# A second level inside product 5 of the last unit of a seven-product matmul kernel

## The chip, the cores and the metric

One core of one Trainium2 chip. The time is device microseconds of that core, the median of several executions.

Times **counted from the first matmul of the last unit** are called "of the unit" below.

## The reference

```python
# x0: [16384, 1024] bf16, ws: [6, 1024, 1024] bf16, bs: [6, 1024] bf16
x = x0
for l in range(6):
    proj = jnp.einsum('bd,de->be', x, ws[l]) + bs[l]
    x = x0 * proj + x
return x
```

## The kernel before

The batch is cut into 16 pairs of blocks of 512 rows. With six layers that makes 96 units (pair, layer). Each unit is one product of 1024 x 1024 by 1024 x 1024, done as a two by two block product with seven half-size products instead of eight (Winograd's form). In 89 units products 5 and 2 are again done by that form (the "second level", seven inner products of a quarter size each). The first pair and the last unit have one level only.

An entry of a rank table, such as `P5.0@6.9`, gives an operation a wished time; a list scheduler orders the instructions of each engine by it. `P` is a group of four matmuls that sum into one bank of PSUM (the memory that TensorE writes), `E` and `F` are ScalarE evacuations of such banks (`F` into another bank), `Q, U, V, W` are the four output quadrants.

```python
def group(name, w, bank, bname, rhs, rname, m, start, u=u):
    def fn():
        for k in range(KH):                                    # KH = 4
            nc.tensor.matmul(bank[:], lhsT=wt[(u, w)][:, k, m * P:(m + 1) * P], rhs=rhs[:, k, :],
                             start=(start and k == 0), stop=(k == KH - 1), skip_group_check=True)
# ... (one: a unit with one level; pA, pX: four PSUM banks each)
for m in range(KH):
    group(f"P1.{m}", "1", pA[m], A[m], B11, [XI[0, 0]], m, True)
    if one:
        copy(f"F1.{m}", pX[m][:], pA[m][:], [A[m]], [Xn[m]])           # product 1 into product 2's bank
        group(f"P2.{m}", "2", pX[m], Xn[m], B21, [XI[1, 0], Xn[m]], m, False)
        biased(f"E2.{m}", Q[:, m, :], pX[m][:], 0, m, [Xn[m]], [f"Q.{m}"])
        group(f"P5.{m}", "5", pX[m], Xn[m], T[1], ["T1"], m, True)
        copy(f"E5.{m}", P5s[:, m, :], pX[m][:], [Xn[m]], [f"5c.{m}"])
# ... second level: inner products on 256 columns in two banks a, b, with ScalarE between them
inner(5, b, True)
copy(X + "e_p5", ip5[X][:], v3(b), [Xn[b]], [X + "ps"])
inner(1, a, True)
copy(X + "f1", pX[b][:], pX[a][:], [Xn[a]], [Xn[b]])
inner(2, b, False)
copy(X + "e_c11", c(0, 0), v3(b), [Xn[b]], cn(0, 0))
inner(6, a, False)
copy(X + "f2", pX[b][:], pX[a][:], [Xn[a]], [Xn[b]])                  # must end before inner 7 writes bank a
inner(3, b, False)
copy(X + "e_c12", iu[X][:, 0], v3(b), [Xn[b]], [X + "u0"])
inner(7, a, False)
# ...
```

In the last unit there is an output stage. Q and the two halves of U are transposed by DMA from the SyncE queue and stored by GpSimd. V and W are transposed on TensorE, evacuated, and stored by four DMAs, the last of them (half of W) from ScalarE's queue.

Of the kernel before, what the change touches and what calls it, by code (L numbers as in the profile page):

```python
# [137 lines left out]
Ua0@16.6 Um0@17.2 Ux0@17.8 Ua1@18.4 Um1@19 Ux1@19.6 Va0@20.4 Vm0@21 Vx0@21.3 Va1@21.6 Vm1@22.2 Vx1@22.8  # L138
Wm0@22.9 Wm1@23.7 Wm2@24.6 Wm3@25.4 cW.0@26.3 cW.1@26.5 cW.2@26.7
trQ@19 stQ@20 trU0@20.5 trU1@22.5 stU0@24 stU1@26 stVa@27 stVb@27.5 stWa@28 stWb@29  # L140
""")}
SPAN2, SPAN0 = 23.4, 24.2

# [2 lines left out]
def kernel(  # L146
# [12 lines left out]
    KH = KD // 2  # L159
# [18 lines left out]
    pA = [psum.tile([P, NB], FP32, name=f"pA{i}") for i in range(KH)]  # L178
    pX = [psum.tile([P, NB], FP32, name=f"pX{i}") for i in range(KH)]
    x0Ts = [work.tile([P, 2, KD, NB], BF16, name=f"x0T{i}") for i in range(2)]  # L180
    xsts = [work.tile([P, 2, KD, NB], BF16, name=f"xst{i}") for i in range(2)]
    T = {i: work.tile([P, KH, NB], BF16, name=f"T{i}") for i in (1, 2, 3, 4)}
# [3 lines left out]
    P1s, P5s, Q, U, V, W = (work.tile([P, KH, NB], BF16, name=f"ev{i}") for i in range(6))  # L186
# [7 lines left out]
    def blk(t, dh, n):  # L194
        return t[:, n, dh * KH:(dh + 1) * KH, :]
# [15 lines left out]
    level1 = lambda u: units[u][0] == 0 or u == NU - 1  # L211
# [3 lines left out]
    for u, (pr, l) in enumerate(units):  # L215
        if pr == 0:
            ring_seq += [(u + 1, w, k) for w, k in RAW if l < L - 1] + [(u, w, k) for w, k in MAKE]
        else:
            order = "1 2 5 6 7 3 4" if level1(u) else "1 5 5i 2 2i 6 3 7 4"
            ring_seq += [(u, w, "load") for w in order.split()]  # L220
    wt, uses_left, live = {}, {}, []
    pos = {"next": 0}
# [44 lines left out]
    for u, (pr, l) in enumerate(units):  # L267
        one, first, last = level1(u), u == 0, u == NU - 1
# [5 lines left out]
        XI = X0 if l == 0 else XO  # L274

        def add(name, fn, rd=(), wr=(), weights=(), rk=rk, base=base, u=u):
            op(base + rk[name], fn, rd, wr, [(u, w) for w in weights])
# [4 lines left out]
        def group(name, w, bank, bname, rhs, rname, m, start, u=u):  # L282
            def fn():
                for k in range(KH):
                    nc.tensor.matmul(bank[:], lhsT=wt[(u, w)][:, k, m * P:(m + 1) * P], rhs=rhs[:, k, :],  # L285
                                     start=(start and k == 0), stop=(k == KH - 1), skip_group_check=True)
            add(name, fn, rname + [f"w{u}.{w}" + ("a" if name in ("P5.0", "P5.1") and u == 0 else "")] if pr == 0 else rname, [bname], [w])

        def copy(name, dst, src, rd, wr):
            add(name, lambda: nc.scalar.copy(out=dst, in_=src), rd, wr)  # L290

        def biased(name, dst, src, eh, m, rd, wr, l=l):
            c = l * KD + eh * KH + m
            add(name, lambda: nc.scalar.activation(out=dst, in_=src, func=IDENT, bias=b_all[:, c:c + 1], scale=1.0), rd, wr)  # L294

        late = []
        if pr == 0:
# [32 lines left out]
            for X, s in (("2i", isum[2 * (l % 2)]), ("5i", isum[2 * (l % 2) + 1])):  # L330
                a = lambda r, c, X=X, u=u: wt[(u, X[0])][:, r * KQ:(r + 1) * KQ, c * HQ:(c + 1) * HQ]
                sv = s[:].rearrange("p q (k e) -> p q k e", k=KQ)
                rn = lambda i, X=X, l=l: f"{X}{l % 2}.{i}"
                src = [f"w{u}.5"] if X == "5i" else []
# [9 lines left out]
        B11, B12, B21, B22 = blk(xs, 0, 0), blk(xs, 0, 1), blk(xs, 1, 0), blk(xs, 1, 1)  # L344
# [3 lines left out]
        ttop("T4", T[4][:], B21, T[2][:], SUB, [XI[1, 0], "T2"], ["T4"])  # L348
        A = [f"A{m}" for m in range(KH)]
        Xn = [f"X{m}" for m in range(KH)]  # L350
        if not one:
            for X, Bm, src in (("5", T[1][:], "T1"), ("2", B21, XI[1, 0])):
                q = lambda dh, n, Bm=Bm: Bm[:, dh * KQ:(dh + 1) * KQ, n * NQ:(n + 1) * NQ]
                t_ = tin[X]
                ttop(X + "t13", t_[:, 0:2], Bm[:, :, NQ:NB].rearrange("p (d k) b -> p d k b", d=2),
                     Bm[:, 0:KQ, :].rearrange("p k (n b) -> p n k b", n=2), SUB, [src], [X + "t13"])
                ttop(X + "t2", t_[:, 2], q(1, 1), t_[:, 0], SUB, [src, X + "t13"], [X + "t2"])
                ttop(X + "t4", t_[:, 3], q(1, 0), t_[:, 2], SUB, [src, X + "t2"], [X + "t4"])
        for m in range(KH):
            group(f"P1.{m}", "1", pA[m], A[m], B11, [XI[0, 0]], m, True)  # L360
            if one:
                copy(f"F1.{m}", pX[m][:], pA[m][:], [A[m]], [Xn[m]])
                group(f"P2.{m}", "2", pX[m], Xn[m], B21, [XI[1, 0], Xn[m]], m, False)
                biased(f"E2.{m}", Q[:, m, :], pX[m][:], 0, m, [Xn[m]], [f"Q.{m}"])
                group(f"P5.{m}", "5", pX[m], Xn[m], T[1], ["T1"], m, True)
                copy(f"E5.{m}", P5s[:, m, :], pX[m][:], [Xn[m]], [f"5c.{m}"])
            else:
                biased(f"E1.{m}", P1s[:, m, :], pA[m][:], 0, m, [A[m]], [f"P1s.{m}"])
        if not one:
            for X, Bm, src, a, b, C in (("5", T[1][:], "T1", 0, 1, P5s), ("2", B21, XI[1, 0], 2, 3, Q)):  # L370
                q = lambda dh, n, Bm=Bm: Bm[:, dh * KQ:(dh + 1) * KQ, n * NQ:(n + 1) * NQ]
                c = lambda dh, n, C=C: C[:, dh * KQ:(dh + 1) * KQ, n * NQ:(n + 1) * NQ]
                cn = (lambda dh, n: [f"5c.{2 * dh}", f"5c.{2 * dh + 1}"]) if X == "5" else (lambda dh, n: [f"Q.{2 * dh}", f"Q.{2 * dh + 1}"])
                t_ = tin[X]

                def inner(i, bank, start, X=X, u=u, q=q, t_=t_):
                    rhs = {1: q(0, 0), 2: q(1, 0), 3: q(1, 1), 4: t_[:, 3], 5: t_[:, 0], 6: t_[:, 2], 7: t_[:, 1]}[i]
                    rn = {1: src, 2: src, 3: src, 4: X + "t4", 5: X + "t13", 6: X + "t2", 7: X + "t13"}[i]
                    w = X if i in (1, 2, 4) else X + "i"

                    def fn():
                        if i in (1, 2, 4):
                            k0, e0 = {1: (0, 0), 2: (KQ, 0), 4: (KQ, HQ)}[i]
                            wv = wt[(u, w)][:, k0:k0 + KQ, e0:e0 + HQ]
                        else:
                            wv = wt[(u, w)][:].rearrange("p q (k e) -> p q k e", k=KQ)[:, {5: 0, 6: 1, 3: 2, 7: 3}[i]]
                        for m in range(KQ):
                            for k in range(KQ):
                                nc.tensor.matmul(pX[bank][:, m * NQ:(m + 1) * NQ], lhsT=wv[:, k, m * P:(m + 1) * P], rhs=rhs[:, k, :],  # L389
                                                 start=(start and m == 0 and k == 0), stop=(k == KQ - 1), skip_group_check=True)  # L390
                    add(X + f"p{i}", fn, [rn, Xn[bank]], [Xn[bank]], [w])

                v3 = lambda bank: pX[bank][:].rearrange("p (m b) -> p m b", m=KQ)
# [7 lines that stand above are left out]
                copy(X + "f2", pX[b][:], pX[a][:], [Xn[a]], [Xn[b]])  # L401
# [3 lines that stand above are left out]
                copy(X + "e_u3", iu[X][:, 1], v3(a), [Xn[a]], [X + "u1"])  # L405
                inner(4, a, False)
                copy(X + "e_c21", c(1, 0), v3(a), [Xn[a]], cn(1, 0))
                ttop(X + "cc", C[:, :, NQ:NB].rearrange("p (d m) b -> p d m b", d=2), iu[X][:],
                     ip5[X][:].unsqueeze(1).to_broadcast([P, 2, KQ, NQ]), ADD, [X + "u0", X + "u1", X + "ps"],
                     cn(0, 1) + cn(1, 1))  # L410
        for m in range(KH):
            xb = m if one else m % 2
            group(f"P6.{m}", "6", pA[m], A[m], T[2], ["T2", A[m]], m, False)
            copy(f"F.{m}", pX[xb][:], pA[m][:], [A[m]], [Xn[xb]])
            group(f"P3.{m}", "3", pX[xb], Xn[xb], B22, [XI[1, 1], Xn[xb]], m, False)
            biased(f"E3.{m}", U[:, m, :], pX[xb][:], 0, m, [Xn[xb]], [f"U.{m}"])
            group(f"P7.{m}", "7", pA[m], A[m], T[3], ["T3", A[m]], m, False)
            biased(f"E7.{m}", V[:, m, :], pA[m][:], 1, m, [A[m]], [f"V.{m}"])
            group(f"P4.{m}", "4", pA[m], A[m], T[4], ["T4", A[m]], m, False)
            if not (last and m == KH - 1):  # L420
                biased(f"E4.{m}", W[:, m, :], pA[m][:], 1, m, [A[m]], [f"W.{m}"])
# [198 lines left out]
```

## Time and profile before

| What | Value |
|---|---|
| time (5 runs) | 2277.06 us median (2276.72 to 2277.62) |
| TensorE | 99% of the span busy, granted clock 1.00 |
| chain that ended last | TensorE 98% |
| one product of the last unit | 3.45 us |
| product 3 starts, of the unit | 13.82 us |
| last store has landed, of the unit | 31.81 us |
| end of the span after that landing | 0.90 us |

The rows that carry this are shown in the prediction.

### The profile page before, as it was taken

How to read it: one execution, taken by the hardware profiler on the slowest of the kernel's cores; microseconds unless marked ns; L12 is line 12 of the kernel's file. 1: busy time of each engine (PE TensorE's matmuls, PEld its weight loads, DVE VectorE, ACT ScalarE, POOL GpSimd, SP SyncE). 2: the span in 40 equal slices, each digit the busy share in tenths (PEclk: the TensorE clock that was granted, in tenths of full speed). 3: DMA queues.
4: the chain of work that ended last, by engine and by line, in shares of the span. 5: the costliest groups of instructions: out<-in, count | busy, mean ns of one | idle time of the engine just before them, and what ended most of it. 6: DMA issues, size and time to landing. Idle time of an engine off the chain costs nothing.

```text
span 2275.4 us, 34743 instructions
## 1 busy us (share of the span) xinstructions
PE 2253.0 (99%) x12713; PEld 1264.4 (56%) x12951; DVE 2080.4 (91%) x2325; ACT 1841.6 (81%) x3228; POOL 24.5 (1%) x46
## 2 busy tenths in 40 slices
PE   9999999999999999999999999999999999999998
PEld 4455555555555555555555555555555555555554
DVE  7999999999999999999999999999999999999997
ACT  5678888888888888888888888888888888888887
POOL 1110000000000000000000000000000000000000
PEclk9999999999999999999999999999999999999999
DMA  9779797796977969779697796978969789696872
GB/s 276 231 268 290 262 248 263 218 303 207 255 254 220 288 218 261 251 224 284 213 261 252 230 284 204 268 250 227 283 203 287 232 232 286 193 297 223 235 245 67
DMA packets 625148, 557.01 MB, mean 245 GB/s; under 512 B 397648, under 2 KB 551248, under 8 KB 624976
## 3 DMA queue, kind: packets, MB, share of 16 engines
q1 hardware_dynamic: 617840, 533.53, 79.1%
q0 software_dynamic: 5488, 19.93, 2.3%
q8 instruction: 101, 1.65, 0.3%
q10 hardware_dynamic: 1648, 1.32, 0.2%
q14 instruction: 71, 0.58, 0.1%
HBM read 436.22 MB, written 52.43 MB: 215 GB/s over the span
## 4 chain that ended last, share of the span: by engine, by line
PE 98%; DVE 1%; issue 1%; SPq 1%; DMA 0%; ACT 0%; DVEq 0%
PE pA L285 57%; PE pX L389 24%; PE pX L285 16%; SPq L536 0%; DVE ev L198 0%; DMA wp<-in_ws_dram 0%; DVE xst L198 0%; DVE T L198 0%; DVE ti L198 0%; PE pA L483 0%; DVE wp L198 0%; SPq L545 0%; PE pX L483 0%; ACT ev L294 0%; DVE x0T L494 0%
## 5 line engine op out<-in xcount | busy, mean ns | idle before, releaser
L285 PEld LDWEIGHTS <-wp 128*128 128x128 bf16 x7904 | 772.7, 98 | 843.4 <-issue 5.0
L285 PE MATMUL pA<-T,wp 128*128 128x512 bf16 x4469 | 1047.4, 379 | 7.5
L294 ACT ACTIVATE ev<-pA,b_all 128x512 bf16<-128x512 f32 x1123 | 705.0, 691 | 210.9 <-PE pA L285 164.8
L389 PEld LDWEIGHTS <-wp 128*128 128x128 bf16 x4984 | 487.0, 98 | 157.0 <-issue 15.6
L198 DVE TENSOR_TENSOR ev<-ev,x0T 128x2048 bf16<-128x2048 bf16 (+2 forms) x483 | 483.0, 1002 | 8.1 <-ACT ev L294 1.5
L198 DVE TENSOR_TENSOR xst<-ev,xst 128x2048 bf16<-128x2048 bf16 x319 | 389.1, 1220 | 18.6 <-DVE ev L198 0.5
L389 PE MATMUL pX<-ti,wp 128*128 128x256 bf16 x2848 | 397.6, 272 | 0.0
L198 DVE TENSOR_TENSOR ev<-ev,ev 128x2048 bf16<-128x2048 bf16 (+1 forms) x283 | 343.9, 1215 | 26.4 <-ACT ev L294 7.6
L294 ACT ACTIVATE ev<-pX,b_all 128x512 bf16<-128x512 f32 x412 | 289.5, 705 | 60.3 <-PE pX L285 49.1
L285 PE MATMUL pX<-xst,wp 128*128 128x512 bf16 x1369 | 335.6, 379 | 0.3
L285 PE MATMUL pA<-xst,wp 128*128 128x512 bf16 x1205 | 302.4, 379 | 4.0
L290 ACT COPY pX<-pA 128x512 f32<-128x512 f32 x412 | 256.4, 625 | 44.5 <-PE pA L285 44.1
L290 ACT CAST ev<-pX 128x512 bf16<-128x512 f32 x384 | 224.9, 619 | 48.0 <-ACT ev L294 37.4
L198 DVE TENSOR_TENSOR ev<-iu,ip 128x1024 bf16<-128x1024 bf16 x178 | 122.6, 689 | 120.7 <-ACT iu L290 120.7
L290 ACT COPY pX<-pX 128x512 f32<-128x512 f32 x356 | 208.7, 587 | 8.3
L290 ACT CAST iu<-pX 128x512 bf16<-128x512 f32 x356 | 197.0, 639 | 0.0
L198 DVE TENSOR_TENSOR T<-xst 128x2048 bf16<-128x2048 bf16 x160 | 194.9, 1218 | 0.3
L198 DVE TENSOR_TENSOR T<-xst,T 128x2048 bf16<-128x2048 bf16 x160 | 195.0, 1219 | 0.0
L389 PE MATMUL pX<-T,wp 128*128 128x256 bf16 x1068 | 160.2, 273 | 0.0
L290 ACT CAST ip<-pX 128x512 bf16<-128x512 f32 x178 | 104.8, 589 | 54.0 <-PE pX L389 54.0
L389 PE MATMUL pX<-xst,wp 128*128 128x256 bf16 x888 | 133.2, 273 | 0.0
L198 DVE TENSOR_TENSOR xst<-ev,x0T 128x2048 bf16<-128x2048 bf16 x64 | 78.3, 1223 | 1.6
(46 smaller groups left out, 627.5 us busy)
## 6 DMA issues: line engine op xcount, KB each, us to landing
wp<-Lc SPq DMA_DIRECT2D x538, 512.0 KB, 4.6
wp<-in_ws_dram SPq DMA_DIRECT2D x285, 512.0 KB, 5.3
out_dram<-x0T SPq DMA_DIRECT2D x30, 1024.0 KB, 8.4
Lc<-wp POOLq DMA_DIRECT2D x24, 512.0 KB, 6.0
Lc<-isum POOLq DMA_DIRECT2D x12, 512.0 KB, 6.8
w<-in_ws_dram SPq DMA_DIRECT2D x5, 512.0 KB, 6.3
wp<-in_ws_dram ACTq DMA_DIRECT2D x2, 512.0 KB, 6.2
out_dram<-x0T SPq DMA_DIRECT2D x3, 256.0 KB, 3.3
```

Source lines behind the costliest of these rows:

```text
L198: nc.vector.tensor_tensor(out=o, in0=a, in1=b, op=op)
L285: nc.tensor.matmul(bank[:], lhsT=wt[(u, w)][:, k, m * P:(m + 1) * P], rhs=rhs[:, k, :], start=(start and k == 0), stop=(k == KH - 1), skip ...
L290: add(name, lambda: nc.scalar.copy(out=dst, in_=src), rd, wr)
L294: add(name, lambda: nc.scalar.activation(out=dst, in_=src, func=IDENT, bias=b_all[:, c:c + 1], scale=1.0), rd, wr)
L389: nc.tensor.matmul(pX[bank][:, m * NQ:(m + 1) * NQ], lhsT=wv[:, k, m * P:(m + 1) * P], rhs=rhs[:, k, :], start=(start and m == 0 and k == ...
```

## The change

Intent: two matmuls' worth less on TensorE in the last unit. Product 5 gets the second level; products 1 and 2 still share PSUM banks as in a unit of one level. The weights' order gets one more load, `5i`, and follows the new order of products.

```diff
+P1.0@0 P1.1@.86 5p5@1.73 5p1@2.16 P1.2@2.6 P2.0@3.46 5p2@4.3 5p6@4.75 P2.1@5.2 5p7@6.07 5p3@6.5 P1.3@6.94 5p4@7.8 P6.0@8.24
+P2.3@9.1 P6.1@9.97 P2.2@10.83 P6.2@11.7 P6.3@12.56
+F1.0@1.07 F1.1@1.93 5e_p5@2.4 5f1@3.03 E2.0@3.7 5e_c11@4.4 5f2@4.9 E2.1@5.4 5e_u3@6.7 5e_c12@7.2 F1.3@8 5e_c21@8.5 F1.2@9 F.0@9.3
+E2.3@10.2 F.1@11 E2.2@11.9 F.2@12.8 F.3@13.6
+T1@-1.14 5t13@.59 5t2@3.06 5t4@5.13 T2@6.93 T3@8.4 T4@10 5cc@11
 ...
-            order = "1 2 5 6 7 3 4" if level1(u) else "1 5 5i 2 2i 6 3 7 4"
+            order = "1 5 5i 2 6 3 7 4" if level1(u) else "1 5 5i 2 2i 6 3 7 4"
 ...
-        if not one:
-            for X, Bm, src in (("5", T[1][:], "T1"), ("2", B21, XI[1, 0])):
+        if not one or last:
+            for X, Bm, src in (("5", T[1][:], "T1"), ("2", B21, XI[1, 0]))[:1 if last else 2]:
 ...
+        if last:
+            second_level([("5", T[1][:], "T1", 2, 3, P5s)])
         for m in range(KH):
 ...
-                group(f"P5.{m}", "5", pX[m], Xn[m], T[1], ["T1"], m, True)
-                copy(f"E5.{m}", P5s[:, m, :], pX[m][:], [Xn[m]], [f"5c.{m}"])
+                if not last:
+                    group(f"P5.{m}", "5", pX[m], Xn[m], T[1], ["T1"], m, True)
+                    copy(f"E5.{m}", P5s[:, m, :], pX[m][:], [Xn[m]], [f"5c.{m}"])
```

More of the change, by code (lines that the diff above doesn't have):

```diff
@@ L358, with second_level @@
                 ttop(X + "t4", t_[:, 3], q(1, 0), t_[:, 2], SUB, [src, X + "t2"], [X + "t4"])
-        for m in range(KH):
-            group(f"P1.{m}", "1", pA[m], A[m], B11, [XI[0, 0]], m, True)
-            if one:
-                copy(f"F1.{m}", pX[m][:], pA[m][:], [A[m]], [Xn[m]])
-                group(f"P2.{m}", "2", pX[m], Xn[m], B21, [XI[1, 0], Xn[m]], m, False)
-                biased(f"E2.{m}", Q[:, m, :], pX[m][:], 0, m, [Xn[m]], [f"Q.{m}"])
-                group(f"P5.{m}", "5", pX[m], Xn[m], T[1], ["T1"], m, True)
-                copy(f"E5.{m}", P5s[:, m, :], pX[m][:], [Xn[m]], [f"5c.{m}"])
-            else:
-                biased(f"E1.{m}", P1s[:, m, :], pA[m][:], 0, m, [A[m]], [f"P1s.{m}"])
-        if not one:
-            for X, Bm, src, a, b, C in (("5", T[1][:], "T1", 0, 1, P5s), ("2", B21, XI[1, 0], 2, 3, Q)):
+        def second_level(which):
+            for X, Bm, src, a, b, C in which:
                 q = lambda dh, n, Bm=Bm: Bm[:, dh * KQ:(dh + 1) * KQ, n * NQ:(n + 1) * NQ]
@@ L410 @@
                      cn(0, 1) + cn(1, 1))
+        five, two = ("5", T[1][:], "T1", 0, 1, P5s), ("2", B21, XI[1, 0], 2, 3, Q)
+        if last:
+            second_level([("5", T[1][:], "T1", 2, 3, P5s)])
+        for m in range(KH):
+            group(f"P1.{m}", "1", pA[m], A[m], B11, [XI[0, 0]], m, True)
+            if one:
+                copy(f"F1.{m}", pX[m][:], pA[m][:], [A[m]], [Xn[m]])
+                group(f"P2.{m}", "2", pX[m], Xn[m], B21, [XI[1, 0], Xn[m]], m, False)
+                biased(f"E2.{m}", Q[:, m, :], pX[m][:], 0, m, [Xn[m]], [f"Q.{m}"])
+                if not last:
+                    group(f"P5.{m}", "5", pX[m], Xn[m], T[1], ["T1"], m, True)
+                    copy(f"E5.{m}", P5s[:, m, :], pX[m][:], [Xn[m]], [f"5c.{m}"])
+            else:
+                biased(f"E1.{m}", P1s[:, m, :], pA[m][:], 0, m, [A[m]], [f"P1s.{m}"])
+        if not one:
+            second_level([five, two])
         for m in range(KH):
```

## The prediction

> **What bounds the kernel now.** I read the page's busy times and its chain that ended last first, then the order of time of the last unit, then half-microsecond windows of the tail.
>
> ```profile
> PE 2253.0 (99%) x12713; PEld 1264.4 (56%) x12951; DVE 2080.4 (91%) x2325; ACT 1841.6 (81%) x3228; POOL 24.5 (1%) x46
> PE 98%; DVE 1%; issue 1%; SPq 1%; DMA 0%; ACT 0%; DVEq 0%
> ```
>
> TensorE is 99% busy and 98% of the chain, with a granted clock of 1.00. A change is therefore worth what it takes from TensorE's stream, less what it puts back as waits. The change touches only the last of the 96 units: the instruction order on every engine is the same up to the second group of that unit, apart from VectorE's order at the border. So the scale is one product of one unit. The timeline by TensorE shows it:
>
> ```profile
> 2242.72 3.62 PE L285 MATMUL pA<-xst,wp 128*128 128x512 bf16 x16
> 2246.18 3.62 PE L285 MATMUL pX<-xst,wp 128*128 128x512 bf16 x15
> 2249.63 3.62 PE L285 MATMUL pX<-T,wp 128*128 128x512 bf16 x16
> 2253.08 3.62 PE L285 MATMUL pA<-T,wp 128*128 128x512 bf16 x16
> ```
>
> The columns are start, length, engine and group. Products 1, 2, 5 and 6 of the last unit follow each other start to start by 3.45 us, with no gap. Product 5 is the third line.
>
> After TensorE's end there is a second stage, which the change can disturb too: outputs are transposed and stored.
>
> ```profile
> 2253.78 1.23 DVE L198 TENSOR_TENSOR xst<-ev,xst 128x2048 bf16<-128x2048 bf16 x1
> 2255.04 10.16 SPq L471 DMA_TRANSPOSE x0T<-xst  x3
> 2262.47 0.77 POOL L474 DMA_DIRECT2D out_dram<-x0T  x1 [2099.52 <-issue]
> 2264.96 0.77 POOL L474 DMA_DIRECT2D out_dram<-x0T  x1 [1.72 <-issue]
> 2268.31 0.75 POOL L474 DMA_DIRECT2D out_dram<-x0T  x1 [2.59 <-DMA x0T<-xst]
> 2270.76 0.39 ACTq L498 DMA_DIRECT2D out_dram<-x0T  x1
> ...
> 2268.00:2268.50 0.50, 0.50 (x13) 0.50 (x10) 0.50 (x3) 0.50 (x2) 0.19 (x1) 1.00 0.00 0
> 2269.50:2270.00 0.50, 0.46 (x9) 0.28 (x6) 0.30 (x2) 0.50 (x2) 0.00 (x0) 1.00 0.96 256
> 2272.00:2272.50 0.50, 0.00 (x0) 0.00 (x0) 0.00 (x0) 0.00 (x0) 0.00 (x0) 1.00 0.95 287
> 2274.00:2274.50 0.50, 0.00 (x0) 0.00 (x0) 0.00 (x0) 0.00 (x0) 0.00 (x0) 1.00 0.21 61
> ```
>
> The first line finishes quadrant Q, which the second transposes; the third to fifth store Q (512 KB) and the halves of U (256 KB each); the sixth is the last store of W. In the windows the last two columns are the DMA share and GB/s: the engines are idle around 2268 to 2269.3, and then full to 2274.2, just ahead of the end at 2275.4. So the last five stores (1.31 MB in some 4.9 us) are bound by transfer, not only by TensorE's last matmul.
>
> **What the Trainium skill says.** "TensorE: Matmul & The Clock Gate", section "Wait — 56ns, not 53.3ns?", gives a warm start-to-start of N ÷ 2.4 GHz plus about 2.5 ns, so 215.8 ns for 512 columns and 109.2 for 256. The trace agrees: 3.45 us over 16 is 215.6 ns, and groups of four 256-column matmuls follow by 0.435 to 0.44 us, about 109 ns each. "PSUM — Partial Sum Buffer", section "PSUM bank collisions raise a hardware error", says to guard PSUM by bank. Here that means that inner product 7 may not write its bank before the ScalarE copy that reads it is done; the trace shows such a pair, a copy from 2228.63 to 2229.27 and the matmul at 2229.32. "Runtime: NRT & Kernel Launch", section "Instruction fetch mechanics", says that a sequencer fetches blocks of 16 KiB over its own DMA queue. This fits the store of Q, which started 3.0 us after the wait before it had ended at 2259.49, with one packet of an instruction queue at 2260.8 between them, while the next stores needed some 0.5 us; the trace does not prove the link. "DMA: Bandwidth & Descriptors", section "Issuing engines are not separate DMA queues", says that all issuers share 16 engines: the tail's shares of 0.93 and more agree.
>
> **The change part by part.**
>
> *Removed from TensorE:* 16 matmuls of 512 columns, 16 x 0.2157 = 3.45 us. *Added:* seven inner products of four 256-column matmuls, 28 x 0.1093 = 3.06 us. **Gain 0.39 us**, or 0.02% of the time. All of it is on the path.
>
> *ScalarE:* four copies of product 5 go, seven come, so three more of about 0.59 us. Its total is far from the bound, but their order matters. I walked it from the start of the unit with durations of the trace. A group's result is read 0.20 us after the next group starts; starts on ScalarE are 0.48 to 0.58 us apart, and 0.62 where one must read what the other overwrites. The order of instructions of the built kernel puts the bias evacuation of product 2, block 0 between the inner copies. TensorE starts that group at 3.46 and the next at 4.32, so ScalarE reads it from 4.52; the cast of the inner corner starts at 4.52 + 0.57 = 5.09; the second inner copy, which overwrites the bank of that cast, at 5.09 + 0.62 = 5.71, and is done at 6.28. Inner product 7 needs it, with 0.05 us for the semaphore: 6.33. TensorE is ready for it at 6.06. **A stall of 0.27 us**, which eats two thirds of the gain. An ordinary second-level unit, where a product 1 evacuation stands there and is ready earlier, has no such stall, as the timeline shows:
>
> ```profile
> 2199.28 0.69 ACT L294 ACTIVATE ev<-pA,b_all 128x512 bf16<-128x512 f32 x1
> 2200.40 0.59 ACT L290 CAST ev<-pX 128x512 bf16<-128x512 f32 x1 [0.42 <-ACT ev L294]
> 2201.02 0.57 ACT L290 COPY pX<-pX 128x512 f32<-128x512 f32 x1
> 2201.89 0.60 PE L389 MATMUL pX<-ti,wp 128*128 128x256 bf16 x4
> ```
>
> There the cast starts 4.58 after the unit's start instead of 5.09 and the copy ends 0.30 before its matmul. Walking on, every later bank is free in time (the last product 2 groups wait for copies that end at 8.9 and 10.0 and start at 9.4 and 11.1).
>
> *VectorE:* T1 moves ahead of the W multiply, into an idle 0.88 us; three small operand subtractions (0.68, 0.42, 0.42 us) and one final add (0.69 us) come. The W sum that product 2 reads ends at about 2245.85, against 2246.18 when it is wanted; T1's first inner operand at about 2243.98, against 2244.45. Tight, but no wait.
>
> *Weights:* one more load of 512 KB, in a stretch with a DMA share of 0.18 and below. Free.
>
> *Q's output:* product 2's last group ends at about 12 us of the unit, not at 6.9, so Q's evacuation ends at 12.9 and its VectorE work starts at 2255.65 instead of 2252.53. **The transpose of Q, and with it its store, move by 3.1 us**: transpose issued at 2258.2, landed at 2262.6, store issued at about 2265.5 if the 3.0 us after the wake come again. The first half of U then queues behind it on the same issuer, to about 2266.8. Data flows some 1.5 us after issue, so 0.79 MB that were written from 2264 to 2267.5 now start at 2267.0 and run into the full stage. Five stores and Q's and U's first half are 2.1 MB; 0.52 at 320 GB/s and 1.57 at 280 take 1.6 + 5.6 = 7.2 us from 2267.0, so to 2274.2 to 2274.5, against 2274.2. The idle 1.3 us at 2268 absorb most of the shift. **Cost 0 to 0.4 us, taken as 0.25.**
>
> *Sum:* TensorE's end moves by -0.39 + 0.27 = -0.12; the store stage, which sets the end, by +0.25, and the 0.12 no longer counts in full there. Net about +0.2: 2276.72 + 0.2 = 2276.9.
>
> **The rivals.** First, *the plain gain*: no stall and no store queue, so -0.4 to 2276.3. For it: TensorE is 98% of the chain, and Q's store is not in the chain. Against it: the walk above finds no slack before inner product 7. Second, *only the stall*: -0.1, to 2276.6, if the store issuer's 3.0 us at the first store do not come again, as then Q is out by 2267. Third, *the store queue in full*: Q and U land on the stores of V and W without filling the gap, 0.5 to 1.2 us more, to 2277.2 to 2277.9. [...]Fourth, *a missed operand*: VectorE is late with the W sum or T1, and product 2 waits some tenths more. I hold the stall with a partly absorbed store queue as likeliest.
>
> **Range and chances.** All the rivals lie within 2276.2 and 2278; the three runs of before spread over 0.9 us by themselves (2276.72 to 2277.62). So 2276.9, with 2276.0 to 2278.1 for 8 in 10. Two per cent would be 45 us, a hundred times the scale of this change: within 2% 0.994, faster 0.003, slower 0.003.
>
> **What would show it.** Right: 28 matmuls of 256 columns more in the last unit; a gap of some 0.2 to 0.4 us on TensorE about 6 us into it, ended by a ScalarE copy within PSUM; product 3 starting 0.1 us earlier within the unit than 13.8; Q's transpose issued near 2258, its store near 2265.5, and no idle DMA windows around 2268. Wrong: no gap there (plain gain), a store of Q within 1 us of its transpose's landing (only the stall), a TensorE wait on VectorE at product 2 (missed operand), or any difference before the last unit, which the order of instructions does not explain.

## The result

The changed kernel took 2277.76 us (median of 5, 2277.01 to 2277.97), against 2277.06 before (median of 5). The ratio is 1.0002, with a 95% interval from 0.9987 to 1.0017. A ratio is the mean time of one kernel's fast runs over that of the other's of the same rounds, so not quite the ratio of the medians.

The page of the changed kernel has the same picture as before:

```profile
PE 2265.5 (100%) x12963; PEld 1265.5 (56%) x12963; DVE 2082.2 (92%) x2329; ACT 1842.6 (81%) x3231; POOL 24.5 (1%) x46
PE 98%; DVE 1%; SPq 0%; DMA 0%; issue 0%; ACT 0%; DVEq 0%
```

The matmul count is no guide to the change here: the first trace of the kernel before lacks some 240 matmul records (12713 against 12951 weight loads), while the changed one's is complete.

In the last unit, which starts at 2241.93 in this trace, the timeline shows the inner products (start, length, engine, line, operation; in brackets the idle time before it and what ended it):

```profile
2246.46 0.69 ACT L299 ACTIVATE ev<-pX,b_all 128x512 bf16<-128x512 f32 x1 [0.87 <-PE pX L290]
...
2247.05 0.58 ACT L295 CAST ev<-pX 128x512 bf16<-128x512 f32 x1
2247.13 1.03 PE L290 MATMUL pX<-xst,wp 128*128 128x512 bf16 x4
2247.66 0.57 ACT L295 COPY pX<-pX 128x512 f32<-128x512 f32 x1
...
2248.28 0.60 PE L384 MATMUL pX<-ti,wp 128*128 128x256 bf16 x4
2248.28 0.75 PEld L384 LDWEIGHTS <-wp 128*128 128x128 bf16 x7 [0.40 <-issue]
```

The group at 2247.13 would be followed at 2248.00. Inner product 7 starts at 2248.28 instead, 0.05 after the copy ends at 2248.23: a stall of 0.28 us. Product 3 starts at 2255.63, which is 13.70 of the unit, 0.12 earlier than before.

The output stage of the changed kernel, in the same view:

```profile
2256.08 1.23 DVE L203 TENSOR_TENSOR xst<-ev,xst 128x2048 bf16<-128x2048 bf16 x1
...
2257.34 6.40 SPq L482 DMA_TRANSPOSE x0T<-xst  x3
...
2264.78 2.27 POOL L485 DMA_DIRECT2D out_dram<-x0T  x3 [2102.59 <-issue]
...
2269.85 0.39 ACTq L509 DMA_DIRECT2D out_dram<-x0T  x1
```

Q's transpose is issued at 15.40 of the unit (12.31 before), its store at 22.84 (19.74 before), and the three GpSimd stores now leave one after another. In half-microsecond windows the transfers are then (last two columns: DMA share, GB/s):

```profile
2265.50:2266.00 0.50, 0.50 (x5) 0.21 (x3) 0.47 (x2) 0.50 (x1) 0.50 (x2) 1.00 0.00 0
...
2267.50:2268.00 0.50, 0.50 (x13) 0.50 (x11) 0.50 (x2) 0.50 (x2) 0.00 (x0) 1.00 0.60 180
...
2273.00:2273.50 0.50, 0.00 (x0) 0.00 (x0) 0.00 (x0) 0.00 (x0) 0.00 (x0) 0.50 0.78 231
```

The idle stretch has moved ahead of the stores (to 2265 to 2266), and data flows to about 2273.5, which is 31.6 of the unit; before it was 2274.2, or 31.5. But the trace goes on to 2275.2. The wait table of SyncE's queue for the last 8 us shows what differs there; first the kernel before, then the changed one (who waited for whom: us in total, times, longest):

```profile
SPq L615 <- DMA out_dram<-x0T: 3.3, 4, 1.5
```

```profile
SPq L626 <- DMA out_dram<-x0T: 3.6, 1, 3.6
```

Before, SyncE waited four times for stores, at most 1.5 us. Now it waits once, for 3.6 us. The single records of these waits and of the stores' completions give, in us of the unit:

```
                      starts of SyncE's end checks                            last landing   end
before    28.14 29.16 29.22 29.29 29.35 29.41 30.03 31.56 31.83                  31.81      32.71
changed   28.33 31.98 32.04 32.10 32.16 32.22 32.29 32.34 32.41                  31.96      33.29
```

A completion semaphore is the counter that tells that a DMA has landed. The checks go through these semaphores in a fixed order, and one takes some 0.06 us. In the kernel before, the last store's semaphore is checked last, so nothing is left to do after it. In the changed kernel it is checked second, and the seven others follow after the landing. The DMAs of SyncE and ScalarE take turns with eight semaphores, and the added weight load has moved every later one of them by one place. (GpSimd's stores have eight others, and kept theirs.)

So the trace says: TensorE -0.12, last landing +0.15, end +0.58.

### The profile page after: what moved, and what is told of

Read it like the earlier page. It is cut to its first block, busy times and chain, and to the rows that moved or that the text cites. A ratio compares the mean times of both kernels' runs of the same rounds, so it can differ in the third digit from the quotient of the medians.

```text
span 2275.2 us, 35017 instructions
## 1 busy us (share of the span) xinstructions
PE 2265.5 (100%) x12963; PEld 1265.5 (56%) x12963; DVE 2082.2 (92%) x2329; ACT 1842.6 (81%) x3231; POOL 24.5 (1%) x46
## 4 chain that ended last, share of the span: by engine, by line
PE 98%; DVE 1%; SPq 0%; DMA 0%; issue 0%; ACT 0%; DVEq 0%
PE pA L290 58%; PE pX L384 24%; PE pX L290 16%; SPq L547 0%; DVE ev L203 0%; DMA wp<-in_ws_dram 0%; DVE xst L203 0%; DVE T L203 0%; DVE ti L203 0%; DVE wp L203 0%; PE pA L494 0%; SPq L556 0%; ACT ev L299 0%; PE pX L494 0%; DVE x0T L505 0%
## 5 line engine op out<-in xcount | busy, mean ns | idle before, releaser
L290 PE MATMUL pA<-xst,wp 128*128 128x512 bf16 x1280 | 313.9, 379 | 0.0
```

## The experiments

All kernels gave correct results. Offsets in us of the unit; "Q transposed" and "Q stored" are the issues of these two DMAs; "end after" is from the last landing to the end of the span.

| Kernel | product 3 | Q transposed | Q stored | last landing | end after | end |
|---|---|---|---|---|---|---|
| before (first trace) | 13.82 | 12.31 | 19.74 | 31.81 | 0.90 | 32.71 |
| before_again | 13.81 | 12.31 | 19.54 | 31.81 | 0.92 | 32.72 |
| changed (first trace) | 13.70 | 15.40 | 22.84 | 31.96 | 1.34 | 33.29 |
| after_again | 13.69 | 15.40 | 22.84 | 31.96 | 1.35 | 33.30 |
| lanes_after | 13.69 | 15.40 | 22.88 | 31.99 | 0.90 | 32.89 |
| lanes_before | 13.81 | 12.31 | 19.72 | 31.80 | 1.33 | 33.13 |
| q_late | 13.81 | 15.52 | 22.98 | 32.09 | 0.90 | 33.00 |
| pool_warm | 13.69 | 15.40 | 20.36 | 31.75 | 1.33 | 33.08 |
| act_order | 13.60 | 15.30 | 22.66 | 31.78 | 1.35 | 33.12 |
| pe_order | 13.48 | 15.18 | 22.63 | 31.74 | 1.35 | 33.08 |
| two_first | (interleaved) | 12.06 | 20.02 | 31.65 | 1.35 | 33.00 |
| two_first_lanes | (interleaved) | 12.06 | 20.01 | 31.66 | 0.90 | 32.57 |
| three_mended | 13.48 | 15.19 | 20.15 | 31.54 | 0.92 | 32.46 |

### before_again: the kernel before, unchanged

> The kernel before once more, unchanged, to see which offsets repeat. Counted from the first matmul of the last unit, the first trace had product 3 at 13.82 us, the landing of the last store at 31.82, the end of the span 0.89 after that landing and 32.71 after the unit's start. If these repeat within 0.1 us, the profile tells differences that the run times (spread 0.9 us) can't; if they scatter by 0.5 us, a single trace of each kernel settles nothing.

Measured: offsets within 0.02 us of the first trace, but for Q's store (0.2 us). The start is another matter: the last unit begins at 2242.72 and 2242.63 in the two traces of the kernel before, at 2241.93 and 2242.93 in those of the changed one. A scatter of up to 1.0 us lies ahead of the last unit, so single times can't tell kernels apart here, while offsets of the unit can. In the two traces of the changed kernel it arises in the first 28 us of the span: the same groups of matmuls start at 26.21 in one and 27.21 in the other, and the distance stays within 0.01 us of that to the last unit.

### after_again: the changed kernel, unchanged

> The changed kernel once more. The first trace had product 3 at 13.70, the last landing at 31.96, the end 1.34 after that landing and 33.30 after the unit's start. Theory (a late Q store, and end checks that come after the last landing): all four repeat within 0.1 us, and the time is 0.6 us over the kernel before. Rival (the 0.7 us between the medians are only the start's scatter, which differed by 0.77 us between the two first traces): the offsets after the last landing scatter, and the times overlap.

Measured: all four offsets repeat within 0.01 us. Time 2277.68 against 2276.96 (medians of 5 and 9), ratio 1.0003 (0.9990 to 1.0017). The rival is out: the 0.6 us at the end belong to the kernel, though the times alone, with this interval, would not show it.

### lanes_after and lanes_before: another place in the turn of semaphores

```diff
-            nc.sync.dma_start(t[:], w_src(units[u][1], w))
+            src = w_src(units[u][1], w)
+            for part in ((slice(0, KQ), slice(KQ, KH)) if w == "4" and u in range(40, 47) else (slice(0, KH),)):
+                nc.sync.dma_start(t[:, part], src[:, part])
```

That is lanes_after, with seven more DMAs in the middle of the run. lanes_before is the kernel before with `u in (40,)`, one more DMA.

> The changed kernel with seven weight loads in the middle split in two, so that the last store gets the last of the eight completion semaphores that take turns, as in the kernel before, and not the first. Theory (the final checks go through the semaphores in a fixed order, some 0.06 us each, and wait at the last store's place): product 3 stays at 13.70, the last landing at 31.96, but the end comes 0.9 us after it instead of 1.34, so 0.45 us less in all. Rival (the longer end belongs to the stores themselves or to the late stores of Q and U): the end stays at 1.34 after the last landing.

> The kernel before with one weight load in the middle split in two, so that its last store gets the first of the eight semaphores. Theory: product 3 stays at 13.82 and the last landing at 31.82, and the end comes 1.34 us after it instead of 0.89: 0.45 us slower with all work the same. Rival: 0.89 as before.

Measured: lanes_after has the landing at 31.99 and the end 0.90 after it; lanes_before 31.80 and 1.33. The wait tables have changed sides as well; first lanes_after, then lanes_before:

```profile
SPq L628 <- DMA out_dram<-x0T: 3.2, 4, 1.3
```

```profile
SPq L617 <- DMA out_dram<-x0T: 3.7, 2, 2.7
```

The times point the same way, but can't show it by themselves: lanes_after 2277.16 and lanes_before 2277.64, against 2276.96 for the kernel before in the same job (ratios 1.0000 and 1.0002, both intervals contain 1). With product 5 and the output stage untouched, one split load somewhere in the middle costs 0.43 us at the end, and seven take it away again. The rival is refuted in both directions.

### q_late: the late Q alone

```diff
+T1@-1.14 P1.0@0 P1.1@.86 P1.2@1.73 P1.3@2.6 P5.0@3.46 P5.1@4.32 P5.2@5.18 P5.3@6.05 P2.0@6.91 P2.1@7.77 P6.0@8.64 P2.3@9.5 P6.1@10.37 P2.2@11.23
+P6.2@12.1 P6.3@12.96
+...
+            if last:
+                group(f"P5.{m}", "5", pX[m], Xn[m], T[1], ["T1"], m, True)
+                copy(f"E5.{m}", P5s[:, m, :], pX[m][:], [Xn[m]], [f"5c.{m}"])
             if one:
                 copy(f"F1.{m}", pX[m][:], pA[m][:], [A[m]], [Xn[m]])
```

> The kernel before with the order of its groups changed so that product 2 ends as late as in the changed kernel (product 5 first in each bank, product 2 between the groups of product 6); no second level, all TensorE work the same. It isolates the late Q. Theory (the late Q store lengthens the store stage by 0.26 us): product 3 at 13.82 as before, Q's transpose issued at about 15.5 us of the unit instead of 12.31, its store at about 23.0 instead of 19.6, the last landing at 32.05 to 32.1 instead of 31.81, the end 0.9 after it. Rival (the late Q is absorbed, and the longer stage comes from something else of the second level): last landing at 31.81.

Measured: product 3 at 13.81, Q's transpose at 15.52, its store at 22.98, last landing at 32.09, end 0.90 after it. So the late Q alone lengthens the way to the last landing by 0.28 us, without any second level. Time 2277.49 against 2277.12 (ratio 1.0002, interval contains 1).

### pool_warm: a tiny GpSimd instruction ahead of its stores

```diff
+            warm = const.tile([P, 1], BF16, name="warm")
+            op(base + 13.7, lambda: nc.gpsimd.tensor_copy(warm[:], T[4][:, 0, 0:1]), ["T4"], ["warm"])
             for nm, src, dst, r, c0, c1 in outs:
```

> The changed kernel with one tiny copy on GpSimd some 9 us into the unit, ahead of the three stores that it issues. It tells what the 3.2 us between the landing of Q's transpose and Q's store are. Theory (a fixed delay of the first instruction after a long sleep): the store follows the landing (19.7 of the unit) within 0.6 us, so at about 20.2 instead of 22.84, and the last landing comes at 31.70, which is 0.26 earlier, as the store stage is no longer crowded. Rival 1 (the delay belongs to the store instruction itself): still 22.84 and 31.96. Rival 2 (the store stage is not crowded by Q): 20.2 but the last landing stays at 31.96.

Measured, in the timeline (the unit starts at 2242.06; first VectorE's last subtraction before the copy, then GpSimd):

```profile
2250.48 1.22 DVE L203 TENSOR_TENSOR T<-xst,T 128x2048 bf16<-128x2048 bf16 x1
2251.77 0.58 POOL L482 COPY warm<-T 128x1 bf16<-128x1 bf16 x1 [2089.10 <-DVE T L203]
2262.42 0.76 POOL L487 DMA_DIRECT2D out_dram<-x0T  x1 [10.07 <-DMA x0T<-xst]
2264.21 0.76 POOL L487 DMA_DIRECT2D out_dram<-x0T  x1 [1.03 <-DMA x0T<-xst]
2267.87 0.75 POOL L487 DMA_DIRECT2D out_dram<-x0T  x1 [2.89 <-DMA x0T<-xst]
```

Q's store leaves at 20.36 instead of 22.84, and the last landing comes at 31.75 instead of 31.96, with TensorE unchanged. Both rivals are out: the delay does not belong to the store itself, and the stage was crowded by Q. But the theory's wording doesn't fit either. The copy is the first instruction after the long idle time, and it starts at 9.71, 0.07 us after the subtraction that it waits for has ended (2251.70, or 9.64). So not everything that comes first is late; what the trace shows is that some 2.5 us of the wait between the landing and Q's store vanish when GpSimd has run something some 10 us before. In the changed kernel a packet of an instruction queue lies at 21.01, between landing and store; with the early copy there is none. That fits an instruction fetch. Nothing here proves it, nor that the queue is GpSimd's, nor that it isn't the added instruction's shift of the code behind it that helps. Time 2277.12 against 2277.12.

### act_order: one evacuation later on ScalarE

```diff
-F1.0@1.07 F1.1@1.93 5e_p5@2.4 5f1@3.03 E2.0@3.7 5e_c11@4.4 5f2@4.9 E2.1@5.4 5e_u3@6.7 5e_c12@7.2 F1.3@8 5e_c21@8.5 F1.2@9 F.0@9.3
+F1.0@1.07 F1.1@1.93 5e_p5@2.4 5f1@3.03 5e_c11@4.4 5f2@4.9 E2.0@5.0 E2.1@5.4 5e_u3@6.7 5e_c12@7.2 F1.3@8 5e_c21@8.5 F1.2@9 F.0@9.3
```

> The changed kernel with product 2's first bias evacuation moved behind the two inner copies on ScalarE. Theory (ScalarE's order makes the stall before inner product 7): the cast starts at 4.96 of the unit instead of 5.12, the copy at 5.58, done at 6.15, inner product 7 at 6.20 instead of 6.35, so half of the stall goes; product 3 at about 13.55 instead of 13.70. Rival (the wait is for something else, such as a weight load or an operand of VectorE): 6.35 and 13.70 stay.

Measured (unit start 2242.18, timeline by ScalarE):

```profile
2247.18 0.58 ACT L295 CAST ev<-pX 128x512 bf16<-128x512 f32 x1 [1.35 <-DVE ti L203]
2247.80 0.57 ACT L295 COPY pX<-pX 128x512 f32<-128x512 f32 x1
```

The cast is at 5.00 of the unit and the copy at 5.62. Inner product 7 starts at 6.25, and product 3 at 13.60. The stall shrank from 0.28 to 0.18, a little less than forecast (0.14). The theory stands: the order on ScalarE makes this stall. (The release named in the bracket is not the true one: the cast reads what inner product 2 had just written.)

### pe_order: another order of groups on TensorE

```diff
-P1.0@0 ... 5p6@4.75 P2.1@5.2 5p7@6.07 5p3@6.5 P1.3@6.94 5p4@7.8 P6.0@8.24
-P2.3@9.1 P6.1@9.97 P2.2@10.83 P6.2@11.7 P6.3@12.56
+P1.0@0 ... 5p6@4.75 P2.1@5.2 P1.3@6.06 5p7@6.92 5p3@7.36 P6.0@7.79 5p4@8.66
+P6.1@9.09 P2.3@9.96 P2.2@10.83 P6.2@11.7 P6.3@12.56
```

(ScalarE's ranks follow in the same order; cut here.)

> The changed kernel with a group of product 1 put between inner products 6 and 7, and one of product 6 between inner products 3 and 4, so that ScalarE has time. Theory: no gap over 0.05 us in the unit, product 3 at 13.43, which is the full 0.39 under the kernel before; the last landing moves by less, to 31.75 to 31.9, as Q is still late and the stores are bound by transfer; the end 1.34 after it. Rival (TensorE's end alone sets the end): last landing at 31.42 + 0.27, which is 31.69.

Measured (unit start 2242.42, timeline by ScalarE, then by TensorE):

```profile
2248.14 0.57 ACT L295 COPY pX<-pX 128x512 f32<-128x512 f32 x1
```

```profile
2248.48 1.03 PE L290 MATMUL pA<-xst,wp 128*128 128x512 bf16 x4
2249.34 0.60 PE L384 MATMUL pX<-ti,wp 128*128 128x256 bf16 x4
```

The copy ends at 2248.71, while TensorE does the inserted group, and inner product 7 starts 0.86 after that group with no gap. One gap of 0.06 is left, before the last product 2 group. Product 3 starts at 13.48, 0.34 before the kernel before, so the arithmetic of 0.39 is right. The last landing is at 31.74: it moved by 0.22, as much as product 3 did (13.70 to 13.48). That is just outside the range the theory gave and nearer the rival. But that doesn't show that TensorE's end sets the landing, because Q's store moved with it (22.84 to 22.63). act_order tells the two apart: there product 3 moved by only 0.10, Q's store by 0.18, and the last landing by 0.18. In all six traces with a late Q and no early GpSimd copy (the changed kernel twice, lanes_after, q_late, act_order, pe_order) the last landing comes 9.11 to 9.12 us after Q's store. So there the stage of stores that Q's store opens sets the last landing, and what TensorE gains counts as far as it brings Q's store forward. With Q's store early (the kernel before twice, lanes_before, pool_warm, three_mended) the last landing follows ScalarE's issue of the last store instead, by 3.76 to 3.84 us. This is read from the traces; no run moves one of the two alone on purpose. The end is 0.21 earlier than in the changed kernel. The time, 2277.89 against 2277.12, does not show it: its scatter is larger than the effect.

### two_first and two_first_lanes: product 2 ahead of the inner products

```diff
+P1.0@0 P1.2@.86 P1.3@1.73 P1.1@2.59 P2.2@3.46 P2.3@4.32 P2.0@5.18 P2.1@6.05 5p5@6.91 5p1@7.35 P6.2@7.79 P6.3@8.65 5p2@9.51 5p6@9.95
+P6.0@10.39 P6.1@11.25 5p7@12.11 5p3@12.55 P3.0@12.99 5p4@13.85 P3.1@14.29 P7.0@15.15 P3.2@16.02 P3.3@16.88 P7.1@17.74 P7.2@18.6 P7.3@19.47
```

(These replace the TensorE ranks; the second level is then declared after product 2. ScalarE's and VectorE's ranks follow. two_first_lanes has the split loads of lanes_after as well.)

> The changed kernel with product 2 ahead of the inner products, which then lie between the groups of product 6, with one of products 3 and 7 each between the last ones. It takes away the stall and the late Q together; the last store still has the first semaphore. Theory: no gap over 0.05 us, products end so that the transposes of V start at 23.78 (24.17 in the kernel before, 24.05 in the changed one), Q's transpose is issued at about 12 us, the last landing at 31.42 to 31.5 (31.81 less 0.39), the end 1.34 after it: 32.8 us after the unit's start, against 32.71 before and 33.30 changed. Rival (a late Q alone is what matters): 31.7.

> The same with seven weight loads in the middle split in two, so that the last store gets the last semaphore. Theory: as the run above up to the landing, then 0.9 us: 32.35 us after the unit's start, which is 0.36 less than the kernel before and 0.95 less than the changed one; in the time that would be 2276.6 against 2277.0, hard to tell within the spread of the runs. Rival: the gain of TensorE's end is lost again in the stores, and the end is at 32.7.

Measured: a miss in part. Q's transpose is at 12.06 as meant, but the last landing is at 31.65, not 31.42 to 31.5. Two new waits appear: 0.20 us before a product 3 group, and at the transposes of V:

```profile
2267.58 0.62 PE L494 MATMUL pX<-ident,ev 128*128 128x128 bf16 x8 [0.58 <-DVE ev L203]
```

The V halves wait for VectorE. It began the first half of U 0.34 us later than in the kernel before (16.80 of the unit against 16.46), because the evacuation that it needs started later (16.07 against 15.74) on a ScalarE without a gap, and it worked without a pause from there. So a part of TensorE's gain became a wait further on. With the last semaphore the end is at 32.57, still 0.14 less than before. Times: 2277.32 and 2276.72, against 2277.22 (ratios 1.0002 and 0.9999, intervals contain 1).

### three_mended: the three costs mended at once

The changed kernel with the edits of pe_order, pool_warm and lanes_after.

> The changed kernel with all three mended at once: the order of groups that had no stall before inner product 7, the tiny GpSimd copy that lets Q's store go out early, and the split loads that give the last store the last semaphore. Theory (the three costs add): TensorE's last transposes of V start at 23.84 as in the run with the new order, the last landing at 31.74 - 0.21 = 31.5, the end 0.9 after it: 32.4 us after the unit's start, 0.3 less than the kernel before and 0.9 less than the changed one. Rival (they overlap, so that what one gives another has given already): 32.65 or more. In the time it would be 0.3 us under the kernel before, which is within the spread of the runs.

Measured: product 3 at 13.48, last landing at 31.54, end 0.92 after it, at 32.46. The three costs add: alone, the three edits bring the end forward by 0.21 (pe_order), 0.21 (pool_warm) and 0.40 us (lanes_after), 0.82 in sum, and together by 0.83. That is also 0.25 less than the kernel before, by offsets. The time is 2276.83 (6 runs), against 2277.24 (10 runs), the right sign, but the ratio 0.9999 (0.9986 to 1.0011) can't confirm it.

## Why the prediction was right or wrong

The measured 2277.76 lies inside the range of 2276.0 to 2278.1, and "within 2%" held. That says little: the range (2.1 us) was wider than the scatter of before's runs (0.9 us), and no change at all or any of the rivals would have lain in it too. Of the 0.86 us between 2276.9 and 2277.76, 0.34 are the base (2276.72, the median of the three runs then known; five give 2277.06). And the size of the difference was off: +0.2 was forecast, and the trace shows +0.58.

- **The arithmetic of TensorE** (0.39 us less) was right: pe_order, with one gap of 0.06 left, starts product 3 at 13.48 instead of 13.81 to 13.82, so 0.39 to 0.40 without that gap.
- **The stall before inner product 7** was right in place, cause and size: cast at 5.12 of the unit (forecast 5.09), copy done at 6.30 (6.28), inner product 7 at 6.35 (6.33). act_order and pe_order show that ScalarE's time between the inner groups is its cause. TensorE's net is -0.12, as forecast. The rival "plain gain" is out.
- **VectorE** was right: the W sum ended at 2245.10, 3.17 of the unit (forecast 3.13), and no TensorE wait came from it. The rival "missed operand" is out.
- **The late Q** was right in its times (transpose at 15.40, forecast 15.4 to 15.5; store at 22.84, forecast about 22.8). Its cost was taken as 0.25; q_late measures 0.28 and pool_warm 0.21. The first half of U left at once after Q, not 0.5 us later as written. The remark that the store stage is what "sets the end" was right for the last landing (9.11 to 9.12 us from Q's store to the last landing in six traces). Wrong is the remark that TensorE's 0.12 "no longer counts in full there": 0.28 - 0.12 is 0.16, and the last landing moved by 0.15. The gain reaches the landing through Q: its store came at 22.84 instead of q_late's 22.98. The rival "store queue in full" is out, and "only the stall" is close to what pool_warm shows once its 0.44 at the end is set aside (last landing 0.06 earlier than before; the rival had 0.1).
- **The step that failed is "Weights: one more load of 512 KB ... Free."** The transfer is indeed free. The load is not, because it is one more DMA in a turn of eight semaphores, and so moves the last store from the last checked to nearly the first. lanes_after and lanes_before measure this term alone as 0.44 to 0.45 and 0.43 us. The working followed the path up to the last landing and took the rest as a constant.
- **A reading that is too strong:** of the "shares of 0.93 and more" in the tail one window is at 0.80 (2271.0 to 2271.5), and high shares alone don't show that the issuers share the engines.

With the end checks the sum is -0.12 + 0.28 + 0.44 = 0.60, against 0.58 measured.

What stays open: what sets the scatter of up to 1 us ahead of the last unit, and why GpSimd's first store is late.

## What to carry to other kernels

When a change is worth tenths of a microsecond, find an offset in the trace that repeats (here to 0.02 us, from a matmul near the end), and judge by that instead of by times that scatter by one. Inner products that hand results on through ScalarE need enough other work between them (here one group of 0.86 us left a stall of 0.28, and two left none). Where an engine's first store after a long idle time comes late, a tiny instruction ahead of it is worth a try (here it brought the store 2.5 us forward). When the end moves with TensorE, look for what else moved with it before calling TensorE the cause. Follow the path past the last landing to the last instruction: here one DMA more decided whether the end checks run before it or after it.

## What the Trainium skill lacked or had wrong

- No page has the checks at the end of the program. "Runtime: NRT & Kernel Launch", section "The ~15µs preamble/postamble breakdown", names a closing barrier of about 1.5 us. Here SyncE goes through the DMA completion semaphores in a fixed order at about 0.06 us each, and the time from last landing to end is 0.90 or 1.34 us by the place of the last store.
- "Runtime: NRT & Kernel Launch", section "Instruction fetch mechanics", calls the fetch mostly hidden. GpSimd, idle for 2100 us, issued its first store 3.15 us after the landing (19.69 to 22.84), with one packet of an instruction queue between, of 8 KiB where the section speaks of 16 KiB blocks. After an early tiny instruction it took 0.69 us (19.67 to 20.36). That it is a fetch is not shown; no page has a delay of this kind.
- "TensorE: Matmul & The Clock Gate", section "Back-to-back issue gap", gives about 131 ns per matmul as sustained for 512 columns in a stream of weight loads and matmuls. Here such a stream runs at 3.45 us for 16, 215.6 ns each, which is the value of the page's formula.
